# Scales of split weights from sums of squares on ScalarE, and high and low halves issued a step apart

## The chip, the cores and the metric

One Trainium2 chip; the kernel runs on one core. The metric is the device time of one execution in microseconds; of several runs of a kernel the median is given.

## The reference

A delta-rule recurrence over 4 x 8 heads of 768 steps gives 3072 tokens of 384 numbers. They pass a mixture of 8 experts in which every token goes to every expert, weighted by a balanced matrix P, and then a second mixture in which every token goes to one expert.

```python
def _moe_ref(x, w_gate, w1, w2):
    ...
    for e in range(E):                      # 8 experts
        h = np.maximum(x @ w1[e], 0.0)      # (3072, 384) @ (384, 1024)
        ye = h @ w2[e]                      # (3072, 1024) @ (1024, 384)
        out += P[:, e:e + 1] * ye
    return out.astype(np.float32)

def _moe2_ref(x, expert_emb, tau, w1, w2):
    ...
    for e in range(E):
        mask = expert_idx == e
        h = np.maximum(x[mask] @ w1[e], 0.0)
        out[mask] = gate_w[mask, None] * (h @ w2[e])
    return out.astype(np.float32)
```

## The kernel before, in words

Float32 operands are held as two float16 parts, high and low, of the operand times a power of two; a product is three matmuls (high x high, high x low, low x high).

The program has these stages. The recurrence runs from 0 to some 600 us together with experts 0 and 1 of the first mixture, in an order that a planner (class `Sched`) writes from costs. A seam up to some 744 us finishes expert 1. Then experts 2 to 6 run in 60 units, twelve for each expert (`units`), each a pair of token tiles of 128. After some 1722 us a second planned stage runs expert 7, the routing and the second mixture.

**Units.** `blocks_first` (line 501) computes the hidden layer of a pair: four buffers `pt`, each from 18 matmuls (L526), are evicted by ScalarE as float32 (`R`, L534) and as the high half (L535); the low half (L536) is put into a list `lows` for VectorE. GpSimd then forms four sums of blocks (`sums`, L517), from which come further operands: `put` gives ScalarE the high half (L513) and VectorE the low one (L514). The function `blocks_second` (line 543) multiplies seven operands of 2x2 blocks with seven of the second weights, 12 matmuls each (L576), into two banks `ta` and `tc_`; VectorE adds results into the output `acc` (L558, L562), and a later product goes on accumulating in the same bank after that. `turned` weaves the second layer of one unit into the first of the next: six steps of the first (18 matmuls), then two products, four times. Each product ends with a hook (`take`), which issues the next entry of the lists `late` (sums 3, 4, 6), `early` (sum 5) or `lows`. VectorE, ScalarE, GpSimd and TensorE each work in the order of issue.

**Preparation.** Beside the units, generators prepare weights: `prep1` the first mixture's next expert, `prep2` the second mixture's experts, whose parts go to the HBM buffer `w2d`. `paced` takes one background step (`bg`) for every BGNS ns of planned TensorE time. `prep_w` (line 366) does a weight matrix (a half of an expert, 128 x 3072 floats in `st`) in steps: load (SyncE's queue), nine empty steps, six maxima of 512 columns (L382), their maximum (L387), the spread of its power of two over the partitions by a diagonal (L358) and a small matmul (`over_parts`, L362, L364), the scale by `pow2` (L332 to L339), and six splits (L343 high on ScalarE, L344 low on VectorE). The second matrix of experts 2 to 6 is cut into blocks of 768 columns instead: `quarters` splits three, subtracts four pairs on GpSimd (L422) and splits the four differences.

Of the kernel before, what the change touches and what calls it, by code (L numbers as in the profile page):

```python
# [9 lines left out]
F32 = mybir.dt.float32  # L10
# [18 lines left out]
FH = KF // 2  # L29
# [201 lines left out]
def kernel(  # L231
# [123 lines left out]
    def over_parts(m1, ma):  # L355
        dg = btok.rearrange("p c a h -> p (c a h)")[:, 0:64].bitcast(BF16)
        nc.vector.tensor_scalar(out=m1.bitcast(U32), in0=m1.bitcast(U32), scalar1=EXPMASK, scalar2=None, op0=ALU.bitwise_and)
        nc.vector.tensor_scalar(out=dg, in0=I128, scalar1=m1, scalar2=None, op0=ALU.mult)  # L358
# [6 lines left out]

    def prep_w(w1, w2, e, W, iv, stages, dst=None, wt=None, mats=None):
        half = WCOLS // 2
        ivs = []
# [5 lines left out]
        for i in range(2):  # L374
            st = stages[i]
            if not apart_:
                load_w(w1, w2, e, i, st)
                for _ in range(9):
                    yield 1
            mx = sm.tile([128, NCH], F32, name="wmx")  # L380
            for c in range(NCH):
                nc.vector.tensor_reduce(  # L382
                    out=mx[:, c:c + 1], in_=st[:, c * CW:c * CW + CW], op=ALU.max, axis=AX.X, apply_absolute_value=True
                )
                yield 1
            m1 = sm.tile([128, 1], F32, name="wm1")
            nc.vector.tensor_reduce(out=m1, in_=mx, op=ALU.max, axis=AX.X)  # L387
            ma = sm.tile([128, 1], F32, name="wma")
            yield from over_parts(m1, ma)
            s, p2 = pow2(ma, 8.0, f"w{i}")  # L390
# [7 lines left out]
            else:  # L398
                for c in range(NCH):
                    a, b = c * CW, c * CW + CW  # L400
                    oh, ol = (wcol(i, c, part) - o for part in range(2))
                    split(st[:, a:b], Wd[:, oh:oh + CW], Wd[:, ol:ol + CW], s)
                    yield 1
            if dst is not None:
                nc.sync.dma_start(out=dst[:, half * i:half * i + half], in_=Wd)
            ivs.append(p2)
        nc.vector.tensor_tensor(out=iv, in0=ivs[0], in1=ivs[1], op=ALU.mult)
        yield 1

    def quarters(st, mats, s):  # L410
# [4 lines left out]
        def put(k, src):  # L415
            hi, lo = (mats[2 * k + part].rearrange("p (f d) -> p f d", f=FH) for part in range(2))
            split(src, hi, lo, s)
        for k, src in enumerate((b11, b21, b22)):
            put(k, src)
            yield 1  # L420
# [5 lines left out]
        for k, src in ((3, b11), (5, b12), (4, b22), (6, b21)):  # L426
            put(k, src)
            yield 1
# [76 lines left out]
    def blocks_first(e, W, r, A, A2, R, R1, solo):  # L505
# [5 lines left out]
        def put(k, src):  # L511
            hi, lo = A[2 * k], A[2 * k + 1]
# [1602 lines left out]
```

## Time and profile before

| | |
|---|---|
| median of 3 runs | 2154.82 us (2151.19 to 2159.76) |
| profiled execution | 2163.61 us, its span 2161.8 us |
| TensorE matmuls busy | 2003.7 us, 93% of the span |
| VectorE busy | 1505.4 us, 70% |
| ScalarE busy | 1039.1 us, 48% |
| GpSimd busy | 615.1 us, 28% |
| mean granted TensorE clock | 0.984 |

The shares are averages over the stages. The first stage waits on long chains, the unit stage on whatever makes TensorE stop, so the table of stretches and the waits of TensorE in one stage say more than the shares. Busy time of matmuls in a stretch can be longer without idle time, at a lower granted clock.

### The profile page before, as it was taken

The page shows a single profiled execution, that of the slowest core. Times are in us where ns is not written, and L with a number is a line of the kernel's source. Part 1 is how long each engine was busy: PE and PEld are TensorE (multiplying, and loading weights), DVE is VectorE, ACT ScalarE, POOL GpSimd, SP SyncE. Part 2 cuts the span into 40 slices and gives each one's busy share as a digit, 9 for nine tenths or more (in the row PEclk, how much of TensorE's full clock was granted, in tenths as well). Part 3 has the DMA queues.
Part 4 walks back from the last instruction along what each step waited for, and adds up shares of the span by engine and source line. Part 5 has one row for each costly group of instructions (what it writes and reads, how often), then busy time and mean ns, then how long its engine had stood idle before and what let it go on. Part 6 is the DMA issues. An engine that isn't in the chain of part 4 may idle for free. (4 is left out here: it accounts for less than half of the span.)

```text
span 2161.8 us, 55457 instructions
## 1 busy us (share of the span) xinstructions
PE 2003.7 (93%) x23391; PEld 1635.6 (76%) x23391; DVE 1505.4 (70%) x3298; ACT 1039.1 (48%) x2038; POOL 615.1 (28%) x524
## 2 busy tenths in 40 slices
PE   3789999999999999999899999999999999999999
PEld 3677777777775588888788888888999855557776
DVE  6988988888664868788778777788876455551111
ACT  6766656656423445444444544445454333332332
POOL 2232233223100223434433433353333201022221
PEclk9989999999999999999999999999999999999999
DMA  8355564555426112021123022111320001167765
GB/s 273 85 101 114 117 123 103 120 114 126 110 81 228 61 60 89 30 98 51 56 92 118 30 89 106 71 60 60 118 89 2 1 23 23 27 216 300 252 230 207
DMA packets 325983, 230.03 MB, mean 106 GB/s; under 512 B 258572, under 2 KB 303536, under 8 KB 319330
## 3 DMA queue, kind: packets, MB, share of 16 engines
q1 hardware_dynamic: 321442, 216.18, 33.8%
q0 software_dynamic: 4288, 10.25, 1.4%
q8 instruction: 185, 3.03, 0.6%
q14 instruction: 68, 0.56, 0.1%
HBM read 146.94 MB, written 50.36 MB: 91 GB/s over the span
## 5 line engine op out<-in xcount | busy, mean ns | idle before, releaser
L526 PE MATMUL pt<-big,W 128*128 128x256 f16 x4320 | 516.5, 274 | 0.0
L526 PEld LDWEIGHTS <-W 128*128 128x128 f16 x4320 | 421.0, 98 | 49.2 <-issue 3.4
L534 ACT ACTIVATE R<-pt 128x512 f32<-128x512 f32 x240 | 142.8, 595 | 462.0 <-PE pt L526 446.6
L517 POOL TENSOR_TENSOR R<-R,R 128x512 f32<-128x512 f32 x120 | 163.0, 1358 | 414.0 <-ACT R L534 302.2
L576 PEld LDWEIGHTS <-A 128*128 128x128 f16 x2520 | 212.1, 98 | 29.7 <-issue 12.3
L517 POOL TENSOR_TENSOR R<-R 128x512 f32<-128x512 f32 x120 | 167.5, 1396 | 203.9 <-ACT R L534 199.2
L1081 PE MATMUL pt<-accb,W 128*128 128x256 f16 (+1 forms) x1368 | 178.0, 269 | 3.6 <-ACT accb L721 1.8
L1107 PE MATMUL py<-W,hhl 128*128 128x384 f16 x756 | 153.6, 330 | 2.7 <-ACT yo L1117 1.8
L576 PE MATMUL py<-W,A 128*128 128x192 f16 x1440 | 137.3, 248 | 14.8 <-DVE accb L558 7.0
L576 PEld LDWEIGHTS <-hhl 128*128 128x128 f16 x1440 | 121.1, 98 | 22.1 <-DVE hhl L536 10.9
L1081 PEld LDWEIGHTS <-W 128*128 128x128 f16 x1368 | 116.1, 99 | 18.4 <-issue 3.9
L1627 PEld LDWEIGHTS <-W 128*128 128x128 f16 x1008 | 90.5, 98 | 51.1 <-issue 0.7
L382 DVE TENSOR_REDUCE wmx<-st 128x1 f32<-128x512 f32 x162 | 104.4, 675 | 29.0 <-DMA st<-in_moe_w_dram 29.0
L558 DVE SCALAR_TENSOR_TENSOR accb<-py,pet,accb 128x192 f32<-128x192 f32 x240 | 116.7, 505 | 7.2 <-PE py L576 7.1
L514 DVE TENSOR_TENSOR A<-R,A 128x512 f16<-128x512 f32 x120 | 98.6, 842 | 32.1 <-ACT A L513 32.0
L1633 DVE SCALAR_TENSOR_TENSOR ttb<-pt,ttb 128x512 f16<-128x512 f32 x50 | 34.6, 691 | 113.2 <-ACT ttb L1632 103.1
L576 PE MATMUL py<-W,hhl 128*128 128x192 f16 x1080 | 105.9, 247 | 7.1 <-DVE hhl L514 7.1
L576 PE MATMUL py<-ew,A 128*128 128x192 f16 x1080 | 104.9, 246 | 4.8 <-DVE A L536 3.3
L1647 PE MATMUL py<-W,hhl 128*128 128x384 f16 x624 | 108.8, 326 | 0.0
L576 PEld LDWEIGHTS <-ttb 128*128 128x128 f16 x1080 | 92.2, 98 | 20.4 <-issue 16.4
L1107 PEld LDWEIGHTS <-hhl 128*128 128x128 f16 x864 | 74.4, 99 | 41.1 <-issue 3.6
L536 DVE SCALAR_TENSOR_TENSOR hhl<-pt,hhl 128x256 f16<-128x256 f32 (+1 forms) x120 | 65.9, 549 | 53.6 <-ACT hhl L535 53.6
(404 smaller groups left out, 4125.5 us busy)
## 6 DMA issues: line engine op xcount, KB each, us to landing
st<-in_moe_w_dram SPq DMA_DIRECT2D x27, 1536.0 KB
W<-w2d SPq DMA_DIRECT2D x18, 1536.0 KB
w2d<-big SPq DMA_DIRECT2D x16, 1536.0 KB
big<-w2d SPq DMA_DIRECT2D x8, 1536.0 KB
accb<-w2d SPq DMA_DIRECT2D x8, 1536.0 KB
big<-accb SPq DMA_DIRECT2D x90, 128.0 KB
accb<-in_kq_dram SPq DMA_DIRECT2D x23, 448.0 KB
st<-PTc SPq DMA_DIRECT2D x42, 128.0 KB
```

The source lines that it names most:

```text
L382: nc.vector.tensor_reduce(out=mx[:, c:c + 1], in_=st[:, c * CW:c * CW + CW], op=ALU.max, axis=AX.X, apply_absolute_value=True)
L514: nc.vector.tensor_tensor(out=lo, in0=src, in1=hi, op=ALU.subtract)
L517: nc.gpsimd.tensor_tensor(out=out, in0=a, in1=b, op=op)
L526: nc.tensor.matmul(out=po, lhsT=w1v(W, wv, kk, f), rhs=xv[:, kk].rearrange("p (h n) -> p h n", h=2), start=kk == 0 and x == 0 and f % 2 == ...
L534: nc.scalar.activation(out=(R1, R)[y][:, :, o:o + 256], in_=pv if y else pv_, func=AF.Relu)
L536: lows.append(lambda pv=pv, hi=hi, lo=lo: nc.vector.scalar_tensor_tensor(out=lo, in0=pv, scalar=0.0, in1=hi, op0=ALU.max, op1=ALU.subtract))
L558: nc.vector.scalar_tensor_tensor(out=acc[t][:, sl], in0=src, scalar=sc, in1=acc[t][:, sl], op0=ALU.mult, op1=ALU.add)
L576: nc.tensor.matmul(out=py, lhsT=A[2 * ka + a_][:, 128 * q_:128 * q_ + 128], rhs=B[2 * kb + b_][:, DH * q_:DH * q_ + DH], start=first and q ...
L1081: nc.tensor.matmul(out=o[g4][:, nt_ * j:nt_ * j + nt_], lhsT=w1v(W, wv, kk, f_), rhs=XR[:, xv, kk], start=(kk == 0 and x == 0), stop=(kk = ...
L1107: nc.tensor.matmul(out=o["py", j][:, 0:DM], lhsT=a_[f_ // per][:, c_:c_ + 128], rhs=w2v(W, b_, f_), start=(f_ == 0 and x == 0), stop=(f_ = ...
L1627: nc.tensor.matmul(out=po, lhsT=w1v(W, wv, kk, f), rhs=xv[:, kk, :], start=(kk == 0 and x == 0), stop=(kk == KD - 1 and x == 2))
L1647: nc.tensor.matmul(out=o["py"][:, 0:DM], lhsT=a_[f // per][:, c_:c_ + 128], rhs=w2v(W, b_, f), start=(f == 0 and x == 0), stop=(f == KF - ...
```

## The change

It has five parts. The maxima on VectorE become squares on ScalarE, whose results go to a buffer in PSUM that nobody reads and whose sums per partition are kept; the power of two comes from the exponent of the largest sum, halved. `over_parts` takes the scale's constant, and the reciprocal and three small operations per scale fall away. The weights' splits go through `split_steps`: a step issues the high half of one piece and the low half of the piece before. Sums of blocks have separate entries for high and low, and the hooks are dealt out anew, behind the additions. The steps before the first piece become 11 instead of 9, and BGNS 1050 instead of 1100.

```diff
-    def over_parts(m1, ma):
+    def over_parts(m1, ma, c_=1.0):
         dg = btok.rearrange("p c a h -> p (c a h)")[:, 0:64].bitcast(BF16)
-        nc.vector.tensor_scalar(out=m1.bitcast(U32), in0=m1.bitcast(U32), scalar1=EXPMASK, scalar2=None, op0=ALU.bitwise_and)
-        nc.vector.tensor_scalar(out=dg, in0=I128, scalar1=m1, scalar2=None, op0=ALU.mult)
+        nc.vector.tensor_scalar(out=dg, in0=I128, scalar1=m1, scalar2=c_, op0=ALU.mult, op1=ALU.mult)
...
+    def split_steps(parts, s):
+        for n_ in range(len(parts) + 1):
+            if n_ < len(parts):
+                src, hi, lo = parts[n_]
+                nc.scalar.activation(out=hi, in_=src, func=AF.Copy, scale=s)
+            if n_:
+                src, hi, lo = parts[n_ - 1]
+                nc.vector.scalar_tensor_tensor(out=lo, in0=src, scalar=s, in1=hi, op0=ALU.mult, op1=ALU.subtract)
+            yield 1
...
-                for _ in range(9):
+                for _ in range(11):
                     yield 1
-            mx = sm.tile([128, NCH], F32, name="wmx")
+            ss = sm.tile([128, NCH], F32, name="wmx")
             for c in range(NCH):
-                nc.vector.tensor_reduce(
-                    out=mx[:, c:c + 1], in_=st[:, c * CW:c * CW + CW], op=ALU.max, axis=AX.X, apply_absolute_value=True
-                )
+                jk = psm.tile([128, CW], F32, name="jk", tag="m1")
+                nc.scalar.activation(out=jk, in_=st[:, c * CW:c * CW + CW], func=AF.Square, scale=2.0 ** 0.5, accum_out=ss[:, c:c + 1])
                 yield 1
             m1 = sm.tile([128, 1], F32, name="wm1")
-            nc.vector.tensor_reduce(out=m1, in_=mx, op=ALU.max, axis=AX.X)
-            ma = sm.tile([128, 1], F32, name="wma")
-            yield from over_parts(m1, ma)
-            s, p2 = pow2(ma, 8.0, f"w{i}")
+            nc.vector.tensor_reduce(out=m1, in_=ss, op=ALU.add, axis=AX.X)
+            nc.vector.tensor_scalar(out=m1, in0=m1, scalar1=1e-36, scalar2=None, op0=ALU.max)
+            nc.vector.tensor_scalar(
+                out=m1.bitcast(U32), in0=m1.bitcast(U32), scalar1=1, scalar2=EXPMASK, op0=ALU.logical_shift_right, op1=ALU.bitwise_and)
+            p2 = sm.tile([128, 1], F32, name=f"w{i}p", tag=f"w{i}1a")
+            yield from over_parts(m1, p2, 2.0 ** 63 * 2.0 / (16.0, 64.0)[i])
+            s = sm.tile([128, 1], F32, name=f"w{i}s", tag=f"w{i}1b")
+            nc.vector.tensor_scalar(
+                out=s.bitcast(U32), in0=p2.bitcast(U32), scalar1=EXPMASK, scalar2=None, op0=ALU.bitwise_xor)
...
-                for c in range(NCH):
-                    a, b = c * CW, c * CW + CW
-                    oh, ol = (wcol(i, c, part) - o for part in range(2))
-                    split(st[:, a:b], Wd[:, oh:oh + CW], Wd[:, ol:ol + CW], s)
-                    yield 1
+                yield from split_steps([(st[:, c * CW:c * CW + CW], *(
+                    Wd[:, wcol(i, c, part) - o:wcol(i, c, part) - o + CW] for part in range(2))) for c in range(NCH)], s)
...
-        for k, src in enumerate((b11, b21, b22)):
-            put(k, src)
-            yield 1
+        yield from split_steps([to(k, src) for k, src in enumerate((b11, b21, b22))], s)
...
-        for k, src in ((3, b11), (5, b12), (4, b22), (6, b21)):
-            put(k, src)
-            yield 1
+        yield from split_steps([to(k, src) for k, src in ((3, b11), (5, b12), (4, b22), (6, b21))], s)
...
-        def put(k, src):
-            hi, lo = A[2 * k], A[2 * k + 1]
-            nc.scalar.copy(out=hi, in_=src)
-            nc.vector.tensor_tensor(out=lo, in0=src, in1=hi, op=ALU.subtract)
+        def high(k, src):
+            return lambda: nc.scalar.copy(out=A[2 * k], in_=src)
+        def low(k, src):
+            return lambda: nc.vector.tensor_tensor(out=A[2 * k + 1], in0=src, in1=A[2 * k], op=ALU.subtract)
-                        early.append(lambda: put(5, r11))
+                        early.extend([high(5, r11), low(5, r11)])
-        late.extend([lambda: put(3, r21), lambda: put(4, r22), lambda: put(6, r12)])
+        late.extend([high(3, r21), high(4, r22), low(3, r21), low(4, r22), high(6, r12), low(6, r12)])
...
-            (0, 0, ta[:, lo_], True, True, lambda: add(t1, lo_, ta[:, lo_], s1), (lows,)),
-            (2, 6, tc_[:, lo_], True, True, None, (late, late)),
-            (3, 3, tc_[:, hi_], True, True, lambda: add(t2, slice(0, DM), tc_[:, 0:DM], s2_), (lows,)),
-            (4, 4, ta[:, lo_], False, True, lambda: add(t1, hi_, ta[:, lo_], s1), ()),
-            (6, 2, tc_[:, hi_], False, True, None, (lows,)),
-            (1, 1, tc_[:, lo_], True, True, lambda: add(t1, slice(0, DM), tc_[:, 0:DM], s1), (early,)),
+            (0, 0, ta[:, lo_], True, True, lambda: add(t1, lo_, ta[:, lo_], s1), (late,)),
+            (2, 6, tc_[:, lo_], True, True, None, (late, late, lows, late)),
+            (3, 3, tc_[:, hi_], True, True, lambda: add(t2, slice(0, DM), tc_[:, 0:DM], s2_), (late,)),
+            (4, 4, ta[:, lo_], False, True, lambda: add(t1, hi_, ta[:, lo_], s1), (lows,)),
+            (6, 2, tc_[:, hi_], False, True, None, (early,)),
+            (1, 1, tc_[:, lo_], True, True, lambda: add(t1, slice(0, DM), tc_[:, 0:DM], s1), (early, lows)),
...
                 if q_ == FH - 1:
-                    take(*hook)
                     if done:
                         done()
+                    take(*hook)
                 yield 247
-    BGNS = 1100
+    BGNS = 1050
```

On VectorE, in a unit with the six maxima of a second weight matrix (prep of an expert of the second mixture; `wmx` and `wm` are the maxima, `big` the buffer of the parts, `hhl`, `A` and `ttb` the operands of the blocks). Before:

```order
L382 TENSOR_REDUCE wmx<-st 128x1
L536 SCALAR_TENSOR_TENSOR hhl<-pt,hhl 128x2x256
L382 TENSOR_REDUCE wmx<-st 128x1
L514 TENSOR_TENSOR ttb<-R_15165,ttb 128x512
L558 SCALAR_TENSOR_TENSOR accb<-py,pet,accb 128x384
L382 TENSOR_REDUCE wmx<-st 128x1 x3
L536 SCALAR_TENSOR_TENSOR hhl<-pt,hhl 128x2x256
L562 SCALAR_TENSOR_TENSOR accb<-py,pet,accb 128x384
L382 TENSOR_REDUCE wmx<-st 128x1
L387 TENSOR_REDUCE wm_16004<-wmx 128x1
L357 TENSOR_SCALAR wm_16004<-wm_16004 128x1
L358 TENSOR_SCALAR btok<-cs,wm_16004 128x128
```

The maxima stand between the low halves and the additions, each behind the one before. With the change, over the same products of the second layer:

```order
L544 SCALAR_TENSOR_TENSOR hhl<-pt,hhl 128x256
L566 SCALAR_TENSOR_TENSOR accb<-py,pet,accb 128x384
L522 TENSOR_TENSOR ttb<-R_15165,ttb 128x512
L544 SCALAR_TENSOR_TENSOR hhl<-pt,hhl 128x2x256
L570 SCALAR_TENSOR_TENSOR accb<-py,pet,accb 128x384
L544 SCALAR_TENSOR_TENSOR hhl<-pt,hhl 128x2x256
L566 SCALAR_TENSOR_TENSOR accb<-py,pet,accb 128x192
L397 TENSOR_REDUCE wm_16029<-wmx 128x1
L398 TENSOR_SCALAR wm_16029<-wm_16029 128x1
L399 TENSOR_SCALAR wm_16029<-wm_16029 128x1
L358 TENSOR_SCALAR btok<-cs,wm_16029 128x128
L522 TENSOR_TENSOR hhl<-R_15165,hhl 128x512
```

The maxima are gone from between L536 and the additions; the additions stand ahead of the low halves; the reduction over the six sums comes after the additions of a product.

On ScalarE, over the same steps (`R` is the float32 copy of a buffer `pt`). Before:

```order
L534 ACTIVATE R<-pt 128x2x256
L535 ACTIVATE hhl<-pt 128x2x256
L513 CAST ttb<-R_15165 128x512
L534 ACTIVATE R<-pt 128x2x256
L535 ACTIVATE hhl<-pt 128x2x256
L534 ACTIVATE R_15164<-pt 128x2x256
L535 ACTIVATE A_15162<-pt 128x256
L513 CAST hhl<-R_15165 128x512
L513 CAST ttb<-R 128x512
L534 ACTIVATE R_15164<-pt 128x2x256
L535 ACTIVATE A_15162<-pt 128x256
L513 CAST ttb<-R 128x512
```

In these steps ScalarE has evictions and high halves of sums alone. With the change, from the same pair of rows on:

```order
L542 ACTIVATE R<-pt 128x2x256
L543 ACTIVATE hhl<-pt 128x2x256
L519 CAST ttb<-R_15165 128x512
L394 ACTIVATE jk,wmx<-st 128x512
L542 ACTIVATE R<-pt 128x2x256
L543 ACTIVATE hhl<-pt 128x2x256
L394 ACTIVATE jk,wmx<-st 128x512 x3
L542 ACTIVATE R_15164<-pt 128x2x256
L543 ACTIVATE A_15162<-pt 128x256
L394 ACTIVATE jk,wmx<-st 128x512
L519 CAST hhl<-R_15165 128x512
L394 ACTIVATE jk,wmx<-st 128x512
```

The squares (`jk,wmx`) stand between the evictions; the high half of sum 3 (`hhl<-R`, L513 before, L519 now) is still behind the first eviction of the next unit, now with squares around it.

On VectorE, where that matrix is split (`w1s` is its scale). Before:

```order
L344 SCALAR_TENSOR_TENSOR big<-st,w1s,big 128x512
L536 SCALAR_TENSOR_TENSOR A_15162<-pt,A_15162 128x256
L558 SCALAR_TENSOR_TENSOR accb<-py,pet,accb 128x384
L558 SCALAR_TENSOR_TENSOR accb<-py,pet,accb 128x192
L344 SCALAR_TENSOR_TENSOR big<-st,w1s,big 128x512 x3
L536 SCALAR_TENSOR_TENSOR A_15162<-pt,A_15162 128x2x256
L344 SCALAR_TENSOR_TENSOR big<-st,w1s,big 128x512
L514 TENSOR_TENSOR A_15162<-R_15164,A_15162 128x512
L558 SCALAR_TENSOR_TENSOR accb<-py,pet,accb 128x384
L344 SCALAR_TENSOR_TENSOR big<-st,w1s,big 128x512
```

The six low halves are spread singly and in a row of three, with low halves of block pairs ahead of the additions. With the change:

```order
L522 TENSOR_TENSOR ttb<-R,ttb 128x512
L566 SCALAR_TENSOR_TENSOR accb<-py,pet,accb 128x192
L544 SCALAR_TENSOR_TENSOR A_15162<-pt,A_15162 128x256
L374 SCALAR_TENSOR_TENSOR big<-st,w1s,big 128x512 x4
L566 SCALAR_TENSOR_TENSOR accb<-py,pet,accb 128x384
L522 TENSOR_TENSOR A_15162<-R_15164,A_15162 128x512
L544 SCALAR_TENSOR_TENSOR A_15162<-pt,A_15162 128x2x256
L374 SCALAR_TENSOR_TENSOR big<-st,w1s,big 128x512 x2
L570 SCALAR_TENSOR_TENSOR accb<-py,pet,accb 128x384
L544 SCALAR_TENSOR_TENSOR A_15162<-pt,A_15162 128x2x256
```

The low halves of the weights are the same six; four of them now stand between two pairs of additions, and the low half of a last block pair behind the addition of its product.

## Rows read from the trace of the kernel before

**Rows 1.** Stretches: from:to, length, busy (count) by engine, PEclk, DMA share, GB/s

```profile
763.46:1635.87 872.41, 819.82 (x8451) 759.39 (x8450) 689.64 (x1271) 422.55 (x805) 329.36 (x230) 0.99 0.21 75
...
1635.87:1650.66 14.79, 14.79 (x159) 13.98 (x157) 7.30 (x13) 5.95 (x13) 5.08 (x5) 1.00 0.00 1
972.66:987.75 15.09, 15.00 (x159) 14.02 (x158) 12.20 (x28) 5.94 (x13) 5.07 (x5) 1.00 0.20 80
...
871.21:890.93 19.72, 16.67 (x160) 15.14 (x159) 15.90 (x26) 8.43 (x16) 14.05 (x9) 0.91 0.00 1
1036.63:1055.47 18.84, 16.60 (x159) 14.88 (x157) 14.12 (x22) 9.52 (x18) 6.39 (x5) 0.91 0.22 86
1070.32:1089.90 19.58, 16.33 (x159) 14.75 (x158) 15.02 (x22) 7.92 (x16) 5.78 (x5) 0.91 0.46 162
1214.84:1235.70 20.86, 17.81 (x159) 16.03 (x158) 15.97 (x26) 8.42 (x16) 14.05 (x9) 0.84 0.00 1
720.00:744.32 24.32, 20.46 (x99) 9.80 (x96) 22.07 (x30) 10.12 (x16) 7.28 (x4) 0.93 0.23 74
```

**Rows 2.** Waits of TensorE, 763.46 to 1635.87: total us, times, longest us

```profile
PE py L576 <- DVE accb L558: 17.7, 24, 3.1
PE py L576 <- DVE hhl L536: 9.5, 6, 3.3
PE py L576 <- DVE A L514: 7.9, 9, 2.4
PE py L576 <- DVE hhl L514: 6.2, 6, 1.3
PE pmx L362 <- DVE btok L358: 4.3, 9, 0.7
PE py L576 <- DVE A L536: 3.3, 4, 1.5
```

**Rows 3.** Groups, 744 to 1722: busy us, mean ns, idle us before

```profile
L382 DVE TENSOR_REDUCE wmx<-st 128x1 f32<-128x512 f32 x156 | 100.4, 675 | 29.0 <-DMA st<-in_moe_w_dram 29.0
...
L362 PE MATMUL pmx<-btok,c 128*128 128x128 bf16 x27 | 5.9, 218 | 4.4 <-DVE btok L358 4.3
...
L337 DVE RECIPROCAL w1s<-w1p 128x1 f32<-128x1 f32 x13 | 2.1, 164 | 0.4
```

**Rows 4.** Waits of VectorE, 744 to 1722: total us, times, longest us

```profile
DVE hhl L536 <- ACT hhl L535: 53.6, 37, 3.4
...
DVE A L514 <- ACT A L513: 32.0, 20, 2.5
DVE wmx L382 <- DMA st<-in_moe_w_dram: 29.0, 13, 4.5
```

**Rows 5.** Single lines: duration in ns, min/median/max, first and last start

```profile
L344 DVE SCALAR_TENSOR_TENSOR big<-st,w0s,big x48: 734/746/1760, 789.0 to 1543.2; 128x512 f16<-128x512 f32 x48
...
L382 DVE TENSOR_REDUCE wmx<-st x162: 667/674/687, 687.3 to 1619.9; 128x1 f32<-128x512 f32 x162
...
L514 DVE TENSOR_TENSOR A<-R,A x120: 672/682/2297, 758.5 to 1702.6; 128x512 f16<-128x512 f32 x120
```

**Rows 6.** Groups of ScalarE: a square with accumulated sum, recurrent stage

```profile
L805 ACT ACTIVATE accb<-accb 128x512 f16<-128x512 f32 x23 | 14.4, 626 | 7.0 <-DMA accb<-in_kq_dram 5.2 <-DVE big L723 1.2 <-DMA V<-in_v_dram 0.6
...
L805 ACT ACTIVATION_READ_ACCUMULATOR accb<-accb 128x1 f32 x23 | 4.4, 191 | 0.0
```

**Rows 7.** Timeline, 876 to 885: start us, us, engine line [idle before <-releaser]

```profile
880.36 4.74 POOL L422 TENSOR_TENSOR st<-st 128x768 f32<-128x768 f32 x2
880.87 2.56 DVE L344 SCALAR_TENSOR_TENSOR W<-st,w1s,W 128x768 f16<-128x768 f32 x1
...
883.34 0.41 DVE L536 SCALAR_TENSOR_TENSOR A<-pt,A 128x256 f16<-128x256 f32 x1
883.68 0.93 DVE L558 SCALAR_TENSOR_TENSOR accb<-py,pet,accb 128x384 f32<-128x384 f32 x2
884.33 0.90 PE L576 MATMUL py<-W,ttb 128*128 128x192 f16 x9 [3.05 <-DVE accb L558]
```

More of the change, by code (lines that the diff above doesn't have):

```diff
@@ L364, in over_parts @@
         nc.vector.tensor_reduce(out=ma, in_=pm, op=ALU.max, axis=AX.X)
+    def split_steps(parts, s):
[7 more added lines that the diff above has]
+            yield 1
     def prep_w(w1, w2, e, W, iv, stages, dst=None, wt=None, mats=None):
         half = WCOLS // 2
-        ivs = []
+        ps_ = []
         apart_ = stages[0] is not stages[1]
@@ L398, in prep_w @@
             else:
-                for c in range(NCH):
-                    a, b = c * CW, c * CW + CW
-                    oh, ol = (wcol(i, c, part) - o for part in range(2))
-                    split(st[:, a:b], Wd[:, oh:oh + CW], Wd[:, ol:ol + CW], s)
-                    yield 1
+                yield from split_steps([(st[:, c * CW:c * CW + CW], *(
+                    Wd[:, wcol(i, c, part) - o:wcol(i, c, part) - o + CW] for part in range(2))) for c in range(NCH)], s)
             if dst is not None:
                 nc.sync.dma_start(out=dst[:, half * i:half * i + half], in_=Wd)
-            ivs.append(p2)
-        nc.vector.tensor_tensor(out=iv, in0=ivs[0], in1=ivs[1], op=ALU.mult)
+            ps_.append(p2)
+        nc.vector.scalar_tensor_tensor(out=iv, in0=ps_[0], scalar=0.25, in1=ps_[1], op0=ALU.mult, op1=ALU.mult)
         yield 1
@@ L413, in quarters, with to @@
         b11, b12, b21, b22 = (q_[:, x, y] for x in range(2) for y in range(2))
-        def put(k, src):
-            hi, lo = (mats[2 * k + part].rearrange("p (f d) -> p f d", f=FH) for part in range(2))
-            split(src, hi, lo, s)
-        for k, src in enumerate((b11, b21, b22)):
-            put(k, src)
-            yield 1
+        def to(k, src):
+            return (src, *(mats[2 * k + part].rearrange("p (f d) -> p f d", f=FH) for part in range(2)))
+        yield from split_steps([to(k, src) for k, src in enumerate((b11, b21, b22))], s)
         for out, a, b in ((b11, b12, b11), (b12, b22, b12), (b22, b22, b11), (b21, b21, b22)):
@@ L509, in blocks_first @@
         r11, r12, r21, r22 = R1[:, 0], R[:, 0], R1[:, 1], R[:, 1]
-        def put(k, src):
-            hi, lo = A[2 * k], A[2 * k + 1]
-            nc.scalar.copy(out=hi, in_=src)
-            nc.vector.tensor_tensor(out=lo, in0=src, in1=hi, op=ALU.subtract)
+        def high(k, src):
+            return lambda: nc.scalar.copy(out=A[2 * k], in_=src)
+        def low(k, src):
+            return lambda: nc.vector.tensor_tensor(out=A[2 * k + 1], in0=src, in1=A[2 * k], op=ALU.subtract)
         def sums(out, a, b, op):
@@ L1529, in second_of @@
                 yield 490
-            take(early, late)
+            take(early, late, late)
     for g in range(GW, NG - 1):
@@ L1578 @@
     while early or late or lows:
-        take(lows, early, late)
+        take(lows, early, late, late)
     paced(second_at(len(units) - 1), BGNS)
```

## The prediction, written before the changed kernel ran

> **What bounds the kernel now.** The recurrent stage before 690 us and the planned tail after 1720 us call nothing that is edited, so both keep their time. The change acts between, above all where experts 2 to 6 run in 60 units of 156 matmuls, each weaving the first layer of one pair of token tiles with the second layer of the pair before. So I read the table of stretches unit by unit. The yardstick is a unit with no preparation of weights beside it: 14.79 us, TensorE busy throughout [rows 1], second row. The first row of that group holds the 54 units with preparation beside them: 872.41 us, where 54 x 14.79 = 798.7 would do. So **the preparation costs 73.7 us**, and that is all the change can act on in this stage. Of it 52.6 us are TensorE idle (872.41 - 819.82) and 21.2 us longer busy time (819.82 - 798.7). In the latter are 26 small matmuls that spread a maximum over the partitions (26 x 218 ns = 5.7 us; the row counts one more, before this stretch [rows 3]), and four units at a granted clock of 0.84 or 0.91 [rows 1], fourth to seventh row: their busy sum is 67.4 us where 59.2 would do, 8.2 us. The 7.3 us left I take for restarts after stalls.
>
> Next the waits of TensorE in that stretch [rows 2]. All long ones are for VectorE: 17.7 us for the weighted additions into the output (L558; a product may not accumulate further in its bank before the addition has read it), 7.9 + 6.2 for low halves of sums of blocks (L514), 9.5 + 3.3 for low halves of the last block pair (L536), 4.3 for the diagonal that the spreading matmul multiplies (L358). That is 48.9 of the 52.6.
>
> Why is VectorE late? Not for the six maxima (675 ns each, 156 of them, 100.4 us [rows 3]) by themselves: the unit from 972.66 to 987.75 holds six maxima and a whole scale and loses 0.3 us against the yardstick, 0.2 of it the small matmul [rows 1], third row. The expensive units hold splits. Each split gives ScalarE the high half and, in the same step, VectorE the low half; VectorE works in order, so it stands until ScalarE is done, with everything behind it: 53.6 us before the L536 low halves of the one buffer, 32.0 before low halves of sums, and 29.0 us at a maximum whose load had not landed [rows 4]. And a low half that overlaps work of GpSimd takes up to 1760 ns instead of 746, one of a sum 2297 instead of 682, while a maximum never leaves 667 to 687 [rows 5].
>
> **The change, part by part.** *Maxima to squares.* VectorE loses 156 x 675 ns = 105 us in the stage. ScalarE gains 156 squares with an accumulated sum; the nearest row is a square of the same 128x512 float form, 626 ns, and 191 ns to read the accumulator [rows 6]: 156 x 817 ns = 127 us at most. ScalarE is busy 422.6 of 872 us [rows 1]; with it some 550, or 63%. Cover is there, since in the yardstick unit ScalarE works 5.95 of 14.79 us. If the cover were gone, a square would hold back an eviction by 0.8 us; in the order three squares stand between two evictions of a block pair, a step of 1.05 us apart.
>
> *Fewer small operations.* Per scale VectorE had nine (reduce, mask, diagonal, reduce, maximum, mask, reciprocal, two multiplications) and keeps six. The three lost cost some 0.16 us each, as the reciprocal's 164 ns [rows 3]: 26 x 0.48 = 12 us of VectorE, in a row before the first split. The added wait of VectorE for the last square lies one step (1.05 us) after the square's issue. Bounds per scale: 0, or one square's 0.8 us (26 x 0.8 = 21 us), and something below nothing because the chain is shorter. I take 0, since the yardstick unit's ScalarE is idle most of the time.
>
> *High and low a step apart.* In the weights' splits the low half of a piece is issued with the high half of the next. In the sums, high 3 moves up to the first product's end, and low 3 follows a product later; low 4, high 6 and low 6, high 5 and low 5 are pulled apart likewise. The additions now stand ahead of the low halves of their step, and three of the four L536 low halves are issued one product later. This removes the waits of VectorE for ScalarE from the places where TensorE needs VectorE within 3 us. The four parallel accumulation banks turn over once per unit, so the later L536 costs nothing there. What is late next is the addition or a low half behind a slow weight split.
>
> *Steps.* A half of an expert takes 28 steps of 1050 ns instead of 25 of 1100: 29.4 against 27.5 us of planned TensorE time, 7% longer. The order shows the last spreading matmul after 56.2 units instead of 54.3 of 60, so it still ends under cover. No transfer is added or moved past another on SP. GpSimd's four subtractions per expert come a step later and, at 2.1 us each, go on slowing VectorE. Two more steps before the first piece give each load 1.65 us more.
>
> *The sum* (TensorE idle, old to new). Additions 17.7 to 5: the longest, 3.1 us, lies behind a weight split of 2.56 us beside a subtraction, which remains, and a low half of 0.41, which no longer stands ahead [rows 7]. Low halves of sums 14.1 to 4: the wait for ScalarE and the pieces of 0.7 us ahead of them go, the slow ones under GpSimd stay. Last block 12.8 to 5.5: its place is unchanged, only the queue ahead is shorter. Diagonal 4.3 unchanged. The rest 3.7 to 1.7. Together 52.6 to 20.5: 32.1 us. Of the 15.5 us of slow clock and restarts the same share (20.5 / 52.6) stays, 6 us: 9.5 us more. **Gain 41.6 us.** The opening, 720 to 744 us, where TensorE works 20.46 of 24.32 us beside a VectorE busy 22.07 [rows 1], in the last row, I price at nothing, between -3 and +3: the preparation loses 12 maxima and the small operations before it, but has three steps more to take (3 x 1.05 us), and the idle time there is 3.9 us. The profiled execution is 2163.6 us (span 2161.8); the median of the runs, 2154.8, is 8.8 below it, and I take the gain from the median: **2113 us**.
>
> **A rule against it.** The maxima's row stays flat while the two of low halves double or triple [rows 5]: what the change takes off VectorE is the one kind of work that never collided. The Trainium skill, SBUF — State Buffer, section "Who interferes with whom", says why: a VectorE instruction with two SBUF inputs contends with a GpSimd instruction that reads SBUF, and a reduction never does. The trace agrees (1760, 2297 and 687 ns at most). By that rule alone the expensive operations are left where they are, which is the first rival.
>
> **The rivals.** *A: GpSimd's collisions hold most of the loss.* The low halves stay long, and standing ahead or behind helps little. For it: the four units of lower clock lose 19.8 us together (79.0 - 59.2 [rows 1]), and a longest wait for an addition shows it [rows 7]. Against: the middle split takes 746 ns, so most meet no collision [rows 5]. Price: those 19.8 us and the 5.7 of small matmuls stay, and half of the 48 left: gain 24, 2131 us. Chance 0.15.
>
> *B: only the maxima count.* Pulling apart just moves the waiting, because the low half still comes due at the same product. Then what goes is what the maxima alone cost, 0.3 us for the six of a half [rows 1], third row: 26 x 0.3 = 8 us, 2147 us. Chance 0.09. That the scale does something else than before changes no time, since a scale is a power of two whatever its size.
>
> *C: ScalarE stands at the load.* A square now waits for the weights to land, where a maximum did, 13 times for 29.0 us, 4.5 at most [rows 4]. ScalarE works in order, and behind the square stands the eviction of the last block pair, then its high half, GpSimd's sums and the next unit's second product, 4 us later. It decides if loads land later than the 11 steps after their issue. If each of 26 halves lost 2 us so, 52 us would be added and the 41.6 gained: 2165 us. Against: the 1.65 us more per load take most of a mean wait of 2.2 us (29.0 / 13). Chance 0.05.
>
> **How the numbers follow.** The forecast has 0.71. Best, only the small matmuls and a sixth of the rest stay: gain 57, 2098 us; worst, gain 24, where A begins. With 5 us of scatter below (the runs lie 3.6 below to 4.9 above their median) and up to where B begins the range is 2093 to 2144. About 0.5%, 11 us, is what a measurement of this kernel can tell from no change. Faster by more than that (below 2144): forecast, A and a third of B, less a little for error: 0.85. Within: most of B and a bit of C, 0.10. Slower: C, 0.05.
>
> **What would show it.** Right: VectorE's busy time down by some 115 us and ScalarE's up by 100 to 127; VectorE's waits for high halves (L513, L343) nearly gone; TensorE's waits for the additions and for L514 under 10 us together; units without splits at 14.8 to 15.1 us and fewer units under clock 1.0. A shows as the same stalls behind low halves of over 1.2 us; C as ScalarE's squares waiting for DMA. Wrong is the forecast if the 60 units still lose over 50 us, or if the stages before 690 or after 1720 us move.

## The result, and the profile after

The changed kernel takes **2103.26 us** (median of 4 runs, 2101.38 to 2104.76); the kernel before took 2157.29 us in its four runs beside them. The ratio is 0.9747, 95% interval 0.9714 to 0.9781: 54.0 us less, where 41.6 were forecast, and inside the forecast range of 2093 to 2144 us. The profiled execution is 2101.4 us, its span 2099.2 us, the mean granted clock 0.989.

First the page of the changed kernel, engines' busy time, share and instructions:

```profile
PE 1985.6 (95%) x23391; PEld 1630.9 (78%) x23391; DVE 1387.7 (66%) x3045; ACT 1150.6 (55%) x2374; POOL 602.3 (29%) x524
```

TensorE does the same 23391 matmuls in 18.1 us less busy time. VectorE has 118 us less to do, ScalarE 112 us more. Then the table of stretches of the changed kernel (columns as in [rows 1]): the 56 units whose preparation lies beside them, a unit without, the three dearest, the opening, the unit stage, the rest.

```profile
761.16:1609.10 847.94, 834.94 (x8763) 782.62 (x8762) 594.65 (x1065) 537.77 (x1141) 326.49 (x238) 1.00 0.22 78
1609.10:1623.89 14.79, 14.79 (x159) 13.98 (x157) 7.43 (x13) 5.95 (x13) 5.07 (x5) 1.00 0.01 1
1014.16:1031.90 17.74, 15.64 (x159) 13.74 (x157) 15.69 (x21) 9.37 (x17) 9.50 (x7) 1.00 0.05 12
1210.72:1229.08 18.36, 15.64 (x158) 13.77 (x157) 15.46 (x21) 9.27 (x17) 9.27 (x7) 1.00 0.14 46
1408.27:1426.54 18.27, 15.29 (x158) 13.87 (x157) 13.73 (x18) 9.16 (x17) 8.51 (x7) 1.00 0.25 87
719.50:743.17 23.67, 18.67 (x98) 9.27 (x96) 21.48 (x26) 10.47 (x17) 7.62 (x4) 1.00 0.23 78
743.17:1665.00 921.83, 904.36 (x9445) 843.92 (x9444) 640.41 (x1160) 567.08 (x1200) 351.27 (x256) 1.00 0.21 73
1665.00:2099.20 434.20, 425.10 (x3436) 285.22 (x3434) 156.07 (x492) 147.49 (x271) 79.61 (x103) 0.99 0.45 159
```

The yardstick unit is the same 14.79 us. Preparation beside the units now costs 847.94 - 56 x 14.79 = 19.7 us where it cost 73.7 [rows 1]: 54.0 us less, as the medians say. Idle time fell from 52.6 to 847.94 - 834.94 = 13.0 us. The longer busy time fell from 21.2 to 6.7 us, of which the small matmuls are 5.8 (26 x 222 ns); no unit is left at a lower granted clock, the four of [rows 1] are gone. Of the 24 units without a low half of a weight, 22 take 14.79 to 14.85 us and two 15.52 and 16.22. Half of what remains, 54.4 - 44.4 = 10.0 us, is in the three units of 17.7 to 18.4 us. The rest of the program is unedited; its 434.2 us against 439.8 is scatter, since from the end of the last whole unit to the end of the span the kernels before and after and the twelve below take 445 to 452 us in no order.

TensorE's waits in the 56 units (total us, times, longest us), against [rows 2]:

```profile
PE py L584 <- DVE accb L566: 4.1, 5, 1.4
PE pmx L362 <- DVE btok L358: 3.6, 8, 1.2
PE py L584 <- DVE hhl L522: 1.8, 2, 1.4
PE py L584 <- DVE ttb L522: 1.6, 5, 0.5
PE py L584 <- DVE A L522: 1.2, 3, 0.5
PE py L584 <- DVE hhl L544: 0.4, 1, 0.4
```

Waits of VectorE, and one of ScalarE, 743 to 1667 us, against [rows 4]:

```profile
DVE accb L566 <- PE py L584: 203.3, 126, 3.2
...
DVE wm L397 <- ACT jk L394: 9.7, 10, 2.7
...
DVE hhl L522 <- ACT hhl L519: 3.8, 4, 1.5
...
DVE A L522 <- ACT A L519: 2.9, 2, 1.5
DVE A L544 <- ACT A L543: 1.4, 2, 1.0
...
ACT jk L394 <- DMA st<-in_moe_w_dram: 11.4, 10, 3.0
```

The roles have turned: VectorE stood for ScalarE's high halves, now it stands for 203 us in front of an addition until TensorE is done with the product (7.1 us before). Single lines, duration in ns min/median/max, against [rows 5]:

```profile
L374 DVE SCALAR_TENSOR_TENSOR big<-st,w0s,big x48: 735/743/1810, 785.2 to 1515.0; 128x512 f16<-128x512 f32 x48
...
L374 DVE SCALAR_TENSOR_TENSOR W<-st,w1s,W x22: 740/1014/2570, 875.8 to 1605.3; 128x768 f16<-128x768 f32 x16, 128x512 f16<-128x512 f32 x6
...
L522 DVE TENSOR_TENSOR A<-R,A x120: 674/691/2052, 759.1 to 1646.3; 128x512 f16<-128x512 f32 x120
...
L394 ACT ACTIVATE jk<-st x156: 600/602/616, 772.7 to 1592.4; 128x512 f32<-128x512 f32 x156
L394 ACT ACTIVATION_READ_ACCUMULATOR jk<-st x156: 185/188/203, 773.2 to 1592.9; 128x1 f32 x156
```

Low halves still meet GpSimd now and then (1810, 2570, 2052 ns). A square is 602 + 188 ns, a little below the row it was priced by [rows 6]. The dear units are those with GpSimd's subtractions (L431), in the timelines of GpSimd and of VectorE before the first of them (start, us, engine line):

```profile
1010.88 2.40 POOL L431 TENSOR_TENSOR st<-st 128x768 f32<-128x768 f32 x1
1014.24 4.02 POOL L431 TENSOR_TENSOR st<-st 128x768 f32<-128x768 f32 x2 [0.96 <-DVE W L374]
...
1009.49 4.60 DVE L374 SCALAR_TENSOR_TENSOR W<-st,w1s,W 128x768 f16<-128x768 f32 x2
...
1014.55 2.05 DVE L522 TENSOR_TENSOR ttb<-R,ttb 128x512 f16<-128x512 f32 x1
```

Two low halves of 1.0 us each take 4.60, the next one of a sum 2.05 instead of 0.68, and TensorE then stops several times for 0.3 to 0.5 us.

### The profile page after: what moved, and what is told of

It is laid out like the page before. It is cut to its first block, busy times and chain, and to the rows that moved or that the text cites. A ratio compares the mean times of both kernels' runs of the same rounds, so it can differ in the third digit from the quotient of the medians.

```text
span 2099.2 us, 55384 instructions
## 1 busy us (share of the span) xinstructions
PE 1985.6 (95%) x23391; PEld 1630.9 (78%) x23391; DVE 1387.7 (66%) x3045; ACT 1150.6 (55%) x2374; POOL 602.3 (29%) x524
## 5 line engine op out<-in xcount | busy, mean ns | idle before, releaser
L534 PE MATMUL pt<-big,W 128*128 128x256 f16 x4320 | 511.0, 273 | 0.0
L525 POOL TENSOR_TENSOR R<-R,R 128x512 f32<-128x512 f32 x120 | 155.3, 1294 | 371.6 <-ACT R L542 288.2
L566 DVE SCALAR_TENSOR_TENSOR accb<-py,pet,accb 128x192 f32<-128x192 f32 x240 | 123.0, 513 | 203.8 <-PE py L584 203.3
L525 POOL TENSOR_TENSOR R<-R 128x512 f32<-128x512 f32 x120 | 161.6, 1346 | 195.3 <-ACT R L542 190.6
L394 ACT ACTIVATE jk<-st 128x512 f32<-128x512 f32 x162 | 98.0, 605 | 13.7 <-DMA st<-in_moe_w_dram 11.4
L1635 PE MATMUL pt<-big,W 128*128 128x512 f16 x432 | 97.7, 379 | 0.0
```

The costliest lines, as they stand in the source:

```text
L394: nc.scalar.activation(out=jk, in_=st[:, c * CW:c * CW + CW], func=AF.Square, scale=2.0 ** 0.5, accum_out=ss[:, c:c + 1])
L525: nc.gpsimd.tensor_tensor(out=out, in0=a, in1=b, op=op)
L534: nc.tensor.matmul(out=po, lhsT=w1v(W, wv, kk, f), rhs=xv[:, kk].rearrange("p (h n) -> p h n", h=2), start=kk == 0 and x == 0 and f % 2 == ...
L566: nc.vector.scalar_tensor_tensor(out=acc[t][:, sl], in0=src, scalar=sc, in1=acc[t][:, sl], op0=ALU.mult, op1=ALU.add)
L1635: nc.tensor.matmul(out=po, lhsT=w1v(W, wv, kk, f), rhs=xv[:, kk, :], start=(kk == 0 and x == 0), stop=(kk == KD - 1 and x == 2))
```

## The experiments

Six theories. **O**, mine: the order counts (low halves a step apart, additions ahead of low halves). **B**: the maxima's time on VectorE counts. **P**: what counts is that 28 steps of 1050 ns are 29.4 us, two units of 14.79, so that the preparation stands still against the units instead of drifting (25 x 1100 ns before). **Place**, formed from the first eleven runs: where in a unit the splits fall counts. **A** and **C**: the prediction's rivals. Each ratio is to runs of the kernel before beside the experiment, whose median moved between 2157 and 2163 us; the changed kernel's ratio is 0.9747. The changed kernel itself repeated within 0.8 us (run 9 amounts to a repeat), so what an edit of it loses is given as the difference from 2103.26 us.

**1. Squares alone.** `e1_only_squares`, on the kernel before:

```diff
-                nc.vector.tensor_reduce(out=mx[:, c:c + 1], ...)
+                nc.scalar.activation(out=jk, ..., func=AF.Square, accum_out=ss[:, c:c + 1])
...
-            s, p2 = pow2(ma, 8.0, f"w{i}")
+            nc.vector.tensor_scalar(out=s.bitcast(U32), ..., scalar1=EXPMASK, op0=ALU.bitwise_xor)
```

> The kernel before, with one part of the change alone: squares on ScalarE in place of the maxima, and the short chain of small operations per scale. Splits, sums, hooks and steps stay as before (25 steps of 1100 ns). Theory O (the gain is the order of low halves and additions): the maxima were not what TensorE waited for, VectorE still stands behind ScalarE's high halves, and ScalarE is fuller now: a gain of 0 to 12 us of the 54 (some 2145 to 2157 us), waits for L536, L514 and L558-type lines still above 35 us together in the units. Theory B (the maxima count): VectorE's 108 us less is the gain; at least 35 us, below 2122 us. Theory P (the phase of preparation against units counts): gain under 5 us, since the steps are those of before.

Measured: 2148.05 us, ratio 0.9945 (0.9925 to 0.9965): 9.7 us less than 2157.73. B falls. VectorE's waits, 743 to 1700 us, show why 105 us less work is worth so little:

```profile
DVE hhl L540 <- ACT hhl L539: 85.1, 55, 3.7
DVE A L518 <- ACT A L517: 62.4, 35, 3.5
```

VectorE uses the time won to stand longer before ScalarE's high halves (53.6 and 32.0 us in [rows 4]).

**2. Maxima back.** `e2_maxima_back`, on the changed kernel: the diff of 1 in reverse.

> The changed kernel, with the maxima and the long chain of small operations put back on VectorE; splits a step apart, the new hooks and 28 steps of 1050 ns stay. Theory O: loses only what the maxima cost by themselves, 8 us as rival B was priced, at most 15: 2105 to 2118 us. Theory B: loses 35 us or more, above 2138 us, and the waits for additions and low halves are back. Theory P: as O, loses under 10 us.

Measured: 2110.52 us (2108.80 to 2111.20), 0.9773 (0.9751 to 0.9795). The ratios' intervals overlap; by the medians 7.3 us are lost. VectorE is busy 1502.8 us again, as before, and nearly the whole gain stands. B falls a second time, and 8 us was its right price.

**3. Halves together.** `e3_splits_together`, on the changed kernel:

```diff
-        for n_ in range(len(parts) + 1):
-            ...
+        for src, hi, lo in parts:
+            nc.scalar.activation(out=hi, in_=src, func=AF.Copy, scale=s)
+            nc.vector.scalar_tensor_tensor(out=lo, in0=src, scalar=s, in1=hi, op0=ALU.mult, op1=ALU.subtract)
+            yield 1
+        yield 1
```

> The changed kernel, with the high and the low half of each weight piece issued in one step again (an empty step at the end keeps their number at 28). Theory O: VectorE stands again behind ScalarE in the 325 splits; the additions behind it come late: 10 to 25 us lost (2113 to 2128 us). Theory B: under 3 us lost. Theory P: under 5 us lost, the halves stay locked to the units.

Measured: 2125.34 us, 0.9843 (0.9821 to 0.9866): 22 us lost. (The weights' splits in the stage are some 160; the 325 of the expectation counts the two halves of each.) VectorE's waits and TensorE's longest, 743 to 1700 us:

```profile
DVE W L370 <- ACT W L369: 19.5, 17, 2.5
DVE big L370 <- ACT big L369: 19.2, 19, 1.9
...
PE py L581 <- DVE accb L563: 11.2, 12, 2.0
```

The wait for the high half is back (38.7 us), and behind it the additions are late (11.2 us, from 4.1). O holds.

**4. Old hooks.** `e4_old_hooks`, on the changed kernel: `put` for both halves of a sum, the old hooks, `take` ahead of `done`.

```diff
-            (2, 6, tc_[:, lo_], True, True, None, (late, late, lows, late)),
+            (2, 6, tc_[:, lo_], True, True, None, (late, late)),
...
+                    take(*hook)
                     if done:
                         done()
-                    take(*hook)
```

> The changed kernel, with the sums' high and low halves together and the hooks of the kernel before, ahead of the additions. Theory O: the low halves of sums and the additions that wait behind them are late again, 14 us of L514's kind and half of the additions' 17.7: 15 to 30 us lost (2118 to 2133 us). Theory B: under 5 us lost, as VectorE has 108 us less to do. Theory P: under 5 us lost.

Measured: 2128.90 us, 0.9854 (0.9822 to 0.9885): 26 us lost. VectorE's longest waits and TensorE's:

```profile
DVE hhl L543 <- ACT hhl L542: 88.5, 63, 3.2
...
DVE A L521 <- ACT A L520: 68.2, 45, 4.3
...
PE py L583 <- DVE accb L565: 16.6, 24, 2.3
```

The additions' waits are back, 16.6 us from 4.1 (17.7 in [rows 2], a somewhat shorter stretch); the sums' low halves wait for ScalarE again, but do not stop TensorE much (2.1 + 1.4 us). O holds.

**5. Additions first, alone.** `e5_additions_first`, on the kernel before:

```diff
-                    take(*hook)
                     if done:
                         done()
+                    take(*hook)
```

> The kernel before, with one part of the order alone: at each product's end the addition is issued ahead of the hook. If the additions were late because of the low half issued just ahead of them (0.4 to 0.7 us, or its wait for ScalarE), TensorE's 17.7 us of waits for additions fall by a third to two thirds: a gain of 5 to 12 us (2145 to 2152 us). If they were late because of the weight splits further ahead, a gain under 3 us, and the low halves pay for it.

Measured: 2167.15 us, 1.0028 (1.0005 to 1.0051): no gain. TensorE's waits for additions fall from 19.5 to 13.1 us (743 to 1720 us in both traces), but those for low halves of L536 and L514 rise from 29.6 to 40.0: in the old order the low half that now stands behind the addition is what is late next.

**6. Another pace.** `e6_pace_1100`, on the changed kernel: `BGNS = 1100`.

> The changed kernel with 1100 ns instead of 1050 per step: 28 steps are 30.8 us, so the preparation drifts against the units of 14.79 us, as it did before (27.5 us). Theory O: the order inside a step and at a product's end is the same, so within 6 us of the changed kernel's 2103 (2099 to 2109). Theory P (the locked phase counts): low halves fall on all places of a unit again; 15 us or more lost, above 2118 us.

Measured: 2124.66 us, 0.9823 (0.9803 to 0.9843): 21 us lost for one number. O's expectation, under 6 us, fails, and P's, 15 us or more, is met here.

**7. Nine empty steps.** `e7_wait_9`, on the changed kernel: `range(9)` for `range(11)`.

> The changed kernel with 9 empty steps ahead of a first piece instead of 11 (26 steps, 27.3 us a half, so the phase drifts). Rival C's mechanism: loads land 9.9 us after issue and 9 steps are 9.45 us, so ScalarE stands at a square in most of 26 halves, 1 to 3 us each; with the evictions behind it the units lose 5 us or more, and ScalarE's waits for the load grow from 11.4 to over 25 us. Theory O: ScalarE's waits grow, but the cover holds: within 4 us of the changed kernel. Theory P: 10 us or more lost.

Measured: 2158.29 us, 0.9972 (0.9955 to 0.9989): nearly the whole gain is gone, with all squares and all of the new order in place. Of ScalarE's waits:

```profile
ACT jk L394 <- DMA st<-in_moe_w_dram: 40.4, 15, 4.7
```

So rival C's wait is there, 40.4 us from 11.4, but the steps (26, 27.3 us) drift as well. 8 to 10 were to part these.

**8. Subtractions on VectorE.** `e8_subs_on_vector`, on the changed kernel: `nc.vector` for `nc.gpsimd` in `quarters`.

> The changed kernel with the four subtractions of an expert's second matrix on VectorE instead of GpSimd (16 operations). Theory A for what is left (GpSimd's subtractions beside two-operand work of VectorE make the three units of 17.7 to 18.4 us that lose 10 us together): those units fall to under 15.8 us, 6 to 10 us gained (2093 to 2097 us). Theory O for what is left (VectorE is simply full there): VectorE takes 4 subtractions of some 1 us per expert more, the units stay over 17 us, and the time is within 3 us of the changed kernel or above it.

Measured: 2100.33 us, 0.9707 (0.9687 to 0.9727): the fastest kernel of all, 2.9 us below the changed one by the medians, with overlapping intervals. The units of the subtractions, and single lines:

```profile
1014.43:1030.95 16.52, 14.96 (x159) 13.93 (x158) 15.04 (x22) 9.27 (x17) 6.78 (x5) 1.00 0.12 36
1210.05:1226.51 16.46, 15.13 (x158) 13.87 (x157) 15.10 (x23) 9.26 (x17) 6.34 (x5) 1.00 0.16 52
...
L374 DVE SCALAR_TENSOR_TENSOR W<-st,w1s,W x22: 734/1006/1169, 874.1 to 1601.1; 128x768 f16<-128x768 f32 x16, 128x512 f16<-128x512 f32 x6
...
L431 DVE TENSOR_TENSOR st<-st x16: 943/959/1911, 879.4 to 1404.5; 128x768 f32<-128x768 f32 x16
```

A's collisions are gone there (2570 ns at most became 1169), but the three units fall only to 16.4 to 16.5, with four more operations of 0.96 us on VectorE in each: between the two theories. The fourth set of subtractions, which cost nothing in the changed kernel, gets dearer: its unit takes 14.79 us in the changed kernel (from 880.83) and 16.67 here (from 879.21). So 5.0 us won and 1.9 lost make the small gain.

**9. The load later.** `e9_load_late`, on the changed kernel:

```diff
+                for _ in range(2):
+                    yield 1
                 load_w(w1, w2, e, i, st)
-                for _ in range(11):
+                for _ in range(9):
```

> The changed kernel with only the load of a first matrix issued two steps (2.1 us) later: two empty steps, the load, nine empty steps, the squares. Every other instruction stays at its step, 28 steps of 1050 ns, so the phase against the units is that of the changed kernel, and the load's window is that of the 9-step kernel that lost 55 us. If the load made that loss (rival C's mechanism): ScalarE waits 35 us or more for loads and 30 us or more are lost (above 2133 us). If the phase made it (the drift of 26 steps): ScalarE waits as long, but under 15 us are lost (2103 to 2118 us).

Measured: 2102.51 us, 0.9724 (0.9685 to 0.9762), and ScalarE waits 10.4 us for loads, not 35: the edit did not do what it was made for. The queue of SyncE, first of the changed kernel, then of this one:

```profile
792.63 0.35 SPq L417 DMA_DIRECT2D w2d<-big  x1
793.07 0.39 SPq L353 DMA_DIRECT2D st<-in_moe_w_dram  x1
```

```profile
793.39 0.35 SPq L419 DMA_DIRECT2D w2d<-big  x1
793.84 0.39 SPq L353 DMA_DIRECT2D st<-in_moe_w_dram  x1
```

In both the load goes out 0.44 us behind the write before it, as soon as the buffer is free. Empty steps hold back only what other engines are given after them. The run shows that the changed kernel repeats, and nothing on loads.

**10. Thirteen empty steps, locked.** `e10_wait_13`, on the changed kernel: `range(13)` and `BGNS = 980`, so that a half is 30 x 980 = 29.4 us as well.

> The changed kernel with 13 empty steps ahead of a first piece instead of 11, and 980 ns per step instead of 1050: 30 steps are 29.4 us again, so a half of preparation is two units as before this edit, while the load has 12.7 us instead of 11.5. Phase theory: the halves stay locked to the units, within 6 us of the changed kernel (2097 to 2109 us). Load theory: ScalarE's 11.4 us of waits for loads go, 2 to 8 us gained. If the place of the splits within a unit counts beside the lock, up to 15 us lost.

Measured: 2153.50 us, 0.9966 (0.9949 to 0.9982): 50 us lost at the same locked length, more than any of the three expectations allowed, while ScalarE's waits for loads fall to 3.5 us (11.4 in the changed kernel). So a wait for loads isn't what makes the loss, and P falls as put: the preparation stands still here too, but elsewhere. Four stretches, two units behind a scale's matmul at place 9 of 156 and two behind one at place 114, and the last of them in the timeline:

```profile
929.23:944.02 14.79, 14.79 (x159) 13.98 (x157) 9.87 (x17) 9.59 (x25) 5.04 (x4) 1.00 0.45 147
944.02:959.51 15.49, 15.02 (x160) 13.95 (x158) 13.33 (x24) 9.89 (x20) 5.58 (x5) 1.00 0.16 65
1244.05:1258.89 14.84, 14.84 (x159) 14.02 (x158) 8.54 (x19) 9.69 (x24) 5.03 (x4) 1.00 0.01 2
1258.89:1278.13 19.24, 16.63 (x160) 15.15 (x158) 13.84 (x19) 9.77 (x20) 6.11 (x5) 0.91 0.42 147
```

```profile
1259.72 3.07 POOL L525 TENSOR_TENSOR R<-R,R 128x512 f32<-128x512 f32 x2 [7.62 <-ACT R L542]
...
1260.93 4.10 DVE L374 SCALAR_TENSOR_TENSOR big<-st,w0s,big 128x512 f16<-128x512 f32 x3
1262.84 2.13 PE L534 MATMUL pt<-big,W 128*128 128x256 f16 x18
...
1265.68 1.46 POOL L525 TENSOR_TENSOR R<-R 128x512 f32<-128x512 f32 x1 [1.20 <-ACT R L542]
...
1265.94 1.75 DVE L522 TENSOR_TENSOR A<-R,A 128x512 f16<-128x512 f32 x1
...
1267.74 1.00 PE L584 MATMUL py<-W,A 128*128 128x192 f16 x10 [2.61 <-DVE A L522]
...
1270.44 2.91 PE L534 MATMUL pt<-big,W 128*128 128x256 f16 x18
```

The weights' low halves stand beside GpSimd's sums of the unit (three take 4.10 us, where 2.2 would do) and in front of the low half of a sum, which meets the next of GpSimd's sums (1.75 us) and is late by 2.61 us; after that the same 18 matmuls take 2.91 us instead of 2.13, and the stretch's granted clock is 0.91.

**11. The kernel before, locked.** `e11_before_1180`: `BGNS = 1180` on the kernel before.

> The kernel before with one number changed: 1180 ns per step instead of 1100. 25 steps are then 29.5 us, two units, so its halves of preparation stop drifting against the units, and a load has 10.6 us instead of 9.9. Theory P (the lock is worth 20 us or more by itself): below 2140 us. Theory O (the lock is worth something only with the new order): within 8 us of the kernel before.

Measured: 2152.69 us, 0.9972 (0.9948 to 0.9997): 6 us less by the ratio, 9 by the medians, where P asked for 20. P falls again.

**12. The steps alone.** `e12_before_steps`, on the kernel before: `range(11)`, an empty step behind each group of splits, `BGNS = 1050`.

> The kernel before (maxima on VectorE, high and low halves together, old hooks) with the steps of the changed kernel alone: 11 empty steps, one empty step behind each group of splits, 1050 ns per step. The scale's small matmuls then stand at the very places among the units' matmuls at which the changed kernel has them. Place theory: what a half of preparation costs depends first on where in a unit its splits fall; in the profile of the kernel before, the 11 halves with their scale behind matmul 69 of a unit or later lose 3.1 us each against 1 to 2 us for the early ones, so early places alone give 15 to 30 us (2127 to 2142 us). Order theory (each part worth what its undoing cost: 7, 22 and 26 us, 55 together): the steps alone give nothing, 2150 to 2162 us.

Measured: 2145.61 us, 0.9921 (0.9900 to 0.9942), 15.6 us less than the 2161.16 beside it: the low end of the place theory's gain of 15 to 30 us, though above its 2142. The order theory's "nothing" falls.

**What places cost.** I counted, in TensorE's order of instructions, how many of a unit's 156 matmuls lie ahead of each scale's small matmul, and took the length of that unit and the next over 2 x 14.79 us as the loss of that half. "Early" is a place up to 66 or from 153 on, "late" the rest; the line was drawn after seeing the losses. The last column is the mean of the 48 low halves `big<-st,w0s` (some 743 ns if nothing is beside them), as in these lines of the changed kernel and of run 10:

```profile
L374 DVE SCALAR_TENSOR_TENSOR big<-st,w0s,big 128x512 f16<-128x512 f32 x48 | 39.1, 850 | 2.3 <-ACT big L371 2.1
```

```profile
L374 DVE SCALAR_TENSOR_TENSOR big<-st,w0s,big 128x512 f16<-128x512 f32 x48 | 46.0, 995 | 0.8 <-ACT big L371 0.8
```

| kernel | order | early: halves, us lost each | late: halves, us each | mean low half, ns |
|---|---|---|---|---|
| before | old | 15, 2.2 | 11, 3.1 | 1046 |
| 11, before at 1180 ns | old | 8, 1.1 | 18, 2.9 | 944 |
| 12, before with new steps | old | 24, 2.1 | 2, 2.8 | 824 |
| after | new | 24, 0.7 | 2, 1.6 | 850 |
| 10, thirteen steps | new | 10, 1.3 | 16, 3.0 | 995 |
| 7, nine steps | new | 12, 2.4 | 14, 3.0 | 1061 |
| 6, 1100 ns | new | 11, 0.7 | 14, 1.3 | 1005 |

At late places runs 7 and 10, in the new order, lose as much as the old order, 3 us a half, and their low halves are a third longer than alone. At early places the new order loses 0.7 us where the old one, at the very same places (12 against after), loses 2.1. In each kernel four halves hold the subtractions and are mostly dearer (up to 7.7 us); without them the early halves lose 0.3 (after), 0.4 (10) and 1.4 us (12), the late ones of run 10 2.8. So within run 10, at one pace, an early place goes with 0.4 and a late one with 2.8 us. Two rows don't fit this alone: the early halves of 7, which also wait for loads, and 6, whose late halves cost 1.3 us though their low halves are as long as in 10.

## Why the prediction was right, step by step

**The outcome** was right: faster, inside the range, by the named waits. What it said would show is there: VectorE's busy time in the unit stage 748.96 to 640.41 us (109 less, forecast 115), ScalarE's 463.64 to 567.08 (103 more, forecast 100 to 127), VectorE's waits for high halves nearly gone, additions and low halves of sums together 8.7 us (under 10).

**The sum** was 12 us too small, in three terms. Last block: 12.8 to 5.5 forecast, 0.4 measured; I took the queue ahead as still there at its unchanged place. Slow clock and restarts: 15.5 to 6 forecast, 0.9 measured (6.7 less the small matmuls' 5.8). I scaled them with the idle time; the four units of lower clock held stops of 2.2 to 3.3 us, and the longest wait is now 1.4 us. That this is the reason isn't shown: run 10 has a unit at 0.91 whose longest stop is 0.9 us. The rest of the waits: 3.7 to 1.7, measured 0.3. The other terms held: additions 17.7 to 4.1 (forecast 5), sums 14.1 to 4.6 (4), diagonal 4.3 to 3.6; the opening, priced at nothing within 3 us, went from 24.32 [rows 1] to 23.67. Idle time fell by 39.6 us (32.1), clock and restarts by 14.6 (9.5): 54.2, less 0.1 for longer small matmuls.

**The step that failed** is the paragraph "Steps." It asked only whether the preparation still ends under cover and gave the two empty steps and the 1050 ns no term. Runs 6, 7 and 10 change nothing else and take back 21, 55 and 50 us, although undoing the squares, the splits and the hooks (runs 2 to 4: 7, 22 and 26 us) adds up to the whole gain already. The order and the squares at the 26 steps of run 7 are worth 0.3%, the steps alone (run 12) 0.8%, together 2.5%: more than the sum of both. (At the 28 steps of 1100 ns of run 6 they are worth 1.8%; at the old 9 empty steps and 1100 ns they were not run.) The price of a step that is moved depends on what it comes to stand beside, and I priced the step and not the place. The forecast gave the whole gain to the order and landed in its range because the steps happened to fall on cheap places, which was luck: the same order with 13 empty steps of 980 ns takes 2153.50 us, outside the range.

**Rival A** was half right. Collisions do hold part of the loss: in the three units of run 8 half of the 10 us went with them. But I said that the change leaves them where they are. It moved them: the mean low half of a weight fell from 1046 to 850 ns although no operation of GpSimd went in the unit stage. Of these 48 low halves, those that meet no operation of GpSimd take at most 752 ns in both traces; those that meet one were 19 of 1509 ns on average and are 15 of 1089. How much of a late place's 3 us is collision and how much the order behind it, no run parts. The Trainium skill, SBUF — State Buffer, section "Who interferes with whom", states that a VectorE instruction with two SBUF inputs contends with a GpSimd instruction that reads SBUF; run 8 agrees, since without the subtractions on GpSimd the longest low half `W<-st,w1s` fell from 2570 to 1169 ns. The inference that the change must leave the contention as it was did not follow from that rule.

**Rival B** has 8 us, and runs 1 and 2 give 9.7 and 7.3. That the price came out was luck: of the 0.3 us a half that it was worked out from, 0.2 were the small matmul, which stays, so the row itself gave some 3 us. **Rival C**'s wait is real (11.4 us at 11 steps, 40.4 at 9), and the two added steps keep it small. What it costs by itself stays open: run 9 left the loads where they were, and run 7 has both.

Open too is why 1100 ns a step make the late places cheaper (1.3 us against 3.0). A step of 1100 ns leaves VectorE more room between two low halves than one of 980 or 1050, which would explain it; no run changed that alone.

## What to carry to other kernels

Where background work is woven into a loop by a step counter, look first at where in the loop its expensive steps fall, and whether that place drifts: print the place and the loss of each period side by side, since one number of the pace can be worth as much as a rewritten order. An operation taken off an engine that waits in order can buy little, as 105 us of maxima bought 7 to 10 here with the waits and without them. To take out the waits, pull producer and consumer a step apart, and put what the bottleneck waits for ahead of what it doesn't. Test such parts both ways, alone on the old kernel and taken out of the new one, because gains of this kind don't add.

## What the runs showed of the hardware

- The subtraction of 128x768 floats takes 0.96 us on VectorE (median of 16) and 2.20 us on GpSimd in the changed kernel (run 8 against after). Moving it still gained only 2.9 us.
- The diagonal on VectorE (L358, 128x128 bfloat16 from a stored identity) is 286 ns at least and reached 990 ns in the changed kernel (667 before); the eleven there that took over 300 ns all overlapped a sum of GpSimd (L525).
- A load left 0.44 us behind the write in the same queue, whether two empty steps stood ahead of it in the program or not (run 9).
